# Loads of keys, values and weights issued as two halves: partitions 0 to 63 by SyncE, 64 to 127 by ScalarE

## The chip, the core and the metric

The kernel runs on one core of a Trainium2 chip. The metric is device time in microseconds; the kernel before takes 1985.83 us, the median of three runs.

## What is computed

One decode step goes through four attention layers, A, B, A, B, each added to a running x of 640 values. A and B have their own caches and weights, and in A the repetition of heads is 1, so both compute the same:

```python
q = (layernorm(x) @ wq).reshape(1, 1, 32, 192).transpose(0, 2, 1, 3)
scores = einsum("bhqd,bhkd->bhqk", q, k_cache) * 192 ** -0.5   # k_cache: 1 x 32 x 8192 x 192
p = softmax(scores, axis=-1)
o = einsum("bhqk,bhkd->bhqd", p, v_cache)
x = x + o.transpose(0, 2, 1, 3).reshape(1, 1, 32 * 192) @ wo   # wq 640 x 6144, wo 6144 x 640
```

All inputs are bf16. Each cache has 100.7 MB (32 x 8192 x 192 x 2 bytes), each weight 7.9 MB. Both caches of A and of B are read twice, once for each layer that uses them, but for a few parts that stay on the chip between two layers.

## The kernel before

Heads are worked in pairs, 16 pairs to a layer. A pair's keys lie in the on-chip memory as 128 partitions: 0 to 63 hold the first head, 64 to 127 the second, and each partition holds 128 positions of 192 values, a contiguous row of 49152 bytes in DRAM too. Values lie likewise. The buffer `pool` is cut into eight slots of 24576 bytes per partition (NSLOT), so that a pair's keys or values take two slots (a "whole" load of 6144 KB, line 369), or one for each half (3072 KB, line 371).

For each pair, VectorE multiplies the keys with the query (line 543, into the place of the keys), TensorE sums the products over the 192 values by matmuls with an identity (lines 556 and 58, into S), VectorE reduces the rest (565) and finds the maximum (567, 574), ScalarE takes the exponentials (580), TensorE multiplies with the values (620 and 58, into OY), VectorE gathers the result (638, 639), TensorE sums it into one row (650), and ScalarE writes that row, divided by the sum of exponentials (661). ScalarE also copies the query of the next pair (502). After five, ten and fifteen pairs TensorE multiplies the output rows with a part of wo (513).

The program is written for each engine as a `Queue`: a list of waits and instructions in order, put out at the end (lines 708 to 713). Each engine works through its own list in order. An operation returns an event, a semaphore and the count it will have reached, and others wait for that. Loads come from the list `plan`. `ahead()` (line 394) is called after each step of the computation: it takes loads from the plan as long as the instructions that free their slots have already been put into TensorE's list (`freed`), and `transfer` (336) puts each into SyncE's list, `SP`, with a wait for those instructions. So all 181 loads go through SyncE's one queue, in the order of the plan, and each raises its slot's semaphore `semS` by 16 when it has landed. One small transfer is ScalarE's: x (line 410), the first instruction of its list. The result goes out by SyncE (line 704).

Of the kernel before, what the change touches and what calls it, by code (L numbers as in the profile page):

```python
# [63 lines left out]
PAIRS_W = 5  # L64
# [4 lines left out]
def build(nc, A_x, A_k, A_v, A_wq, A_wo, B_x, B_k, B_v, B_wq, B_wo, out):  # L69
    _, H, SK, DH = A_k.shape  # L70
    D = A_x.shape[-1]
    P = 128
    J = 2 * SK // P
    JU = J // 2
    DC = D // P
# [6 lines left out]
    PD = 2 * DH  # L82
    NW = PAIRS_W * PD // P
    QC = (NPAIR - 1) * PD
    QR = QC // 3
    TS = JU * DH
    QW = H * DH
    Q_PARTS = [(0, 2), (2, 2), (4, 1)]
    OI = PD // P
    NB = [0, 5, 0, 5]  # L90
# [4 lines left out]
                    wo=[NPAIR - PAIRS_W, 1, 1 + PAIRS_W], wol=0)  # L95
    ORDER = [FORWARD, FORWARD, FORWARD, BACKWARD]

    with ExitStack() as ctx:
        def sb(name, shape, dt):
            return ctx.enter_context(nc.sbuf_tensor(name, shape, dt))  # L100
# [4 lines left out]
        def sem(name):  # L105
            return ctx.enter_context(nc.semaphore(name))

        ident = sb("ident", [P, P], BF16)
        pool = sb("pool", [P, NSLOT * TS], BF16)
        slot = [pool[:, i * TS:(i + 1) * TS] for i in range(NSLOT)]  # L110
        wq0 = [sb(f"wq0{i}", [P, DC, PD], BF16) for i in range(2)]
        rows = sb("rows", [P, QR], BF16)
# [52 lines left out]
        AC = Queue(sem("pACT"))  # L165
        PO = Queue(sem("pPOOL"))
        SP = Queue()
        semS = [sem(f"semS{i}") for i in range(NSLOT)]
        semOL, semOB, semVQ, semX, semOUT = [sem(n) for n in ("semOL", "semOB", "semVQ", "semX", "semOUT")]

        e = PO.op(lambda g: g.memset(ident[:], 0.0))
# [5 lines left out]
        e = PO.op(lambda g: g.memset(mask, 0.0))  # L177
        for t in range(G):
            e = PO.op(lambda g, t=t: g.affine_select(
                out=mask, in_=mask, compare_op=ALU.not_equal, fill=1.0,  # L180
                base=-32 * t, pattern=[[-1, 2], [-2, VK]], channel_multiplier=1), e)
# [10 lines left out]
        def pair(l, p):  # L192
            return ORDER[l]["pairs"][p]
# [11 lines left out]
        def whole(kind, l, p):  # L205

            if kind == "t":
                return False
            if kind == "k":
                return l < 2 and p not in (PAIRS_W, 2 * PAIRS_W) or l == 3 and p > 1  # L210
            if p == NPAIR - 1:
                return False
            return l != 2 or p not in (0, PAIRS_W, 2 * PAIRS_W)
# [7 lines left out]
        for l in range(NL):  # L221
# [8 lines left out]
            for p in range(NPAIR):  # L230
# [17 lines left out]
                if p < NPAIR - 2:  # L248
                    if first_load("v", l, p) == (l, p):
                        plan += [("v", l, p, u) for u in range(2)]  # L250
                        if l == 2 and p == 1:
                            i = plan.index(("k", l, 1, 0))
# [31 lines left out]
        place, before, holder = {}, {}, [None] * NSLOT  # L284
# [40 lines left out]
        def wq_rows(l, g):  # L325

            c0, k = Q_PARTS[g]
            if l < 2:
                i = place[("wq", l, 0)] * TS
                return pool[:, i + c0 * QW:i + (c0 + k) * QW].rearrange("p (c n) -> p c n", c=k)  # L330
            return slot[place[("wq", l, g)]][:, 0:k * QC].rearrange("p (c n) -> p c n", c=k)

        def quarters(n):
            return n[0] == "v" and n[2:] == (NPAIR - 1, 1) and NB[n[1]] > 0

        def transfer(n):
            l = n[1]
            o = ORDER[l]
            w = W[l % 2]
            free = [freed[b] for b in before[n]]  # L340
            if n[0] == "wol":
                r0 = o["wol"] * PD
                return SP.op(lambda s: s.dma_start(
                    rows[:], w["wo"][r0:r0 + PD].rearrange("(p i) n -> p (i n)", p=P)),
                    *free, sem=semOL, inc=16)
            if n[0] == "t":
                return max(free, key=lambda e: e[1]) if free else None
            if n[0] == "wob":
                r0 = o["wo"][2] * PD
                return SP.op(lambda s: s.dma_start(  # L350
                    slot[place[("wo", l, 2)]][:, (NW - NB[l]) * D:NW * D],
                    w["wo"][r0:r0 + PAIRS_W * PD].rearrange("(p i) n -> p (i n)", p=P)[:, (NW - NB[l]) * D:]),
                    sem=semOB, inc=16)
            if n[0] == "vq":
                n = ("v", l, NPAIR - 1, 1)
            i = place[n]
            t = slot[i]
            if n[0] in "kv":
                h = 2 * pair(l, n[2])
                r = w[n[0]][0, h:h + 2].rearrange("h (p j) d -> (h p) (j d)", j=J)  # L360
                if quarters(n):
                    x = TS // 2
                    if n in landed:
                        return SP.op(lambda s: s.dma_start(t[:, x:], r[:, TS + x:]), sem=semVQ, inc=16)
                    return SP.op(lambda s: s.dma_start(t[:, 0:x], r[:, TS:TS + x]), *free, sem=semS[i], inc=16)
                if whole(*n[:3]):
                    if n[3] == 1:
                        return landed[n[:3] + (0,)]
                    f = lambda s: s.dma_start(pool[:, i * TS:(i + 2) * TS], r)
                else:  # L370
                    f = lambda s: s.dma_start(t, r[:, n[3] * TS:(n[3] + 1) * TS])
            elif n[0] == "wq" and l < 2:
                f = lambda s: s.dma_start(pool[:, i * TS:i * TS + DC * QW], w["wq"].rearrange("(p c) n -> p (c n)", c=DC))
            elif n[0] == "wq":
                c0, k = Q_PARTS[n[2]]
                f = lambda s: s.dma_start(
                    wq_rows(l, n[2]),
                    w["wq"][:, o["q1"] * PD:o["q1"] * PD + QC].rearrange("(p c) n -> p c n", c=DC)[:, c0:c0 + k, :])
            else:
                r0 = o["wo"][n[2]] * PD  # L380
                k = NW - NB[l] if n[2] == 2 else NW
                f = lambda s: s.dma_start(
                    t[:, 0:k * D], w["wo"][r0:r0 + PAIRS_W * PD].rearrange("(p i) n -> p (i n)", p=P)[:, 0:k * D])
            return SP.op(f, *free, sem=semS[i], inc=16)

        def need(n):

            while n not in landed:
                m = plan[issued[0]]
                issued[0] += 1  # L390
                landed[m] = transfer(m)
            return landed[n]

        def ahead():

            while issued[0] < len(plan):
                m = plan[issued[0]]
                if any(b not in freed for b in before[m]):
                    return
                issued[0] += 1  # L400
                landed[m] = transfer(m)
# [300 lines left out]
        for l in range(NL):  # L702
            ev_z, ev_true = layer(l, ev_z, ev_true)
        e = SP.op(lambda s: s.dma_start(out[0, 0].rearrange("(p c) -> p c", c=DC), x_bf[:]), ev_true, sem=semOUT, inc=16)
        SP.wait(e)
# [10 lines left out]
def bass_interleave_layers__gqa_block_cached__mha_block_cached__decode_kernel(  # L716
    nc: bass.Bass,
    A_x: bass.AP,
    A_k_cache: bass.AP,
    A_v_cache: bass.AP,  # L720
    A_wq: bass.AP,
    A_wo: bass.AP,
    B_x: bass.AP,
    B_k_cache: bass.AP,
    B_v_cache: bass.AP,
    B_wq: bass.AP,
    B_wo: bass.AP,
    out: bass.AP,
):
    build(nc, A_x, A_k_cache, A_v_cache, A_wq, A_wo, B_x, B_k_cache, B_v_cache, B_wq, B_wo, out)  # L730
# [28 lines left out]
```

## Time and profile before

| What | Value |
|---|---|
| Median of three runs | 1985.83 us (1985.55 to 1986.44) |
| The profiled execution's own time | 1985.81 us |
| Its span, first to last instruction | 1984.0 us |
| Mean granted TensorE clock | 0.776 |
| Bytes moved, mean rate | 849.25 MB, 428 GB/s |
| VectorE multiplication of keys (L543) | 512 of 1753 ns, 861.2 us |
| TensorE sums (L58, into S) | 2944 of 425 ns, 789.1 us |
| ScalarE exponentials (L580) | 128 of 435 ns, 55.7 us |

The span is the time within which instructions ran; the profiled execution's own time is 1.8 us more. A busy time is the sum over an engine's instructions. Engines overlap, so these times don't add up to the span. In the groups, "out<-in" names the buffers written and read; SPq and ACTq are the sequencers of SyncE and ScalarE, where loads are issued. In a row of 40 digits each digit is the busy share of a fortieth of the span, in tenths.

### The profile page before, as it was taken

The page shows a single profiled execution, that of the slowest core. Times are in us where ns is not written, and L with a number is a line of the kernel's source. Part 1 is how long each engine was busy: PE and PEld are TensorE (multiplying, and loading weights), DVE is VectorE, ACT ScalarE, POOL GpSimd, SP SyncE. Part 2 cuts the span into 40 slices and gives each one's busy share as a digit, 9 for nine tenths or more (in the row PEclk, how much of TensorE's full clock was granted, in tenths as well). Part 3 has the DMA queues.
Part 4 walks back from the last instruction along what each step waited for, and adds up shares of the span by engine and source line. Part 5 has one row for each costly group of instructions (what it writes and reads, how often), then busy time and mean ns, then how long its engine had stood idle before and what let it go on. Part 6 is the DMA issues. An engine that isn't in the chain of part 4 may idle for free.

```text
span 1984.0 us, 13908 instructions
## 1 busy us (share of the span) xinstructions
PE 1273.4 (64%) x8310; PEld 150.1 (8%) x3266; DVE 1200.7 (61%) x1371; ACT 139.5 (7%) x461; POOL 4.5 (0%) x22
## 2 busy tenths in 40 slices
PE   3567567566466666665775665675676766656657
PEld 0001001000200100100020010010002001001001
DVE  3566467467166656556745565665664775665665
ACT  0000000000000000000010000000000000000000
POOL 0000000000000000000000000000000000000000
PEclk9787777777587787777876777878886887777777
DMA  9999999999999999999999999999999999999998
GB/s 412 438 430 431 431 437 429 431 430 431 433 435 431 432 429 436 430 431 432 427 388 433 430 430 430 432 430 430 431 431 427 435 432 434 430 432 432 432 431 353
DMA packets 26926, 849.25 MB, mean 428 GB/s; under 512 B 3184, under 2 KB 3184, under 8 KB 3952
## 3 DMA queue, kind: packets, MB, share of 16 engines
q1 hardware_dynamic: 26720, 848.38, 99.5%
q8 instruction: 45, 0.74, 0.2%
q14 instruction: 17, 0.14, 0.0%
q10 hardware_dynamic: 144, 0.00, 0.0%
HBM read 848.36 MB, written 0.00 MB: 428 GB/s over the span
## 4 chain that ended last, share of the span: by engine, by line
DMA 68%; DVE 15%; PE 15%; ACT 1%; issue 0%; SPq 0%
DMA pool<-in_B_k_cache_dram 27%; DMA pool<-in_A_v_cache_dram 20%; DMA pool<-in_A_k_cache_dram 14%; DVE pool L543 13%; PE S L58 6%; PE OY L58 5%; DMA pool<-in_B_v_cache_dram 4%; PE OY L620 3%; DMA pool<-in_B_wo_dram 2%; ACT p_sb L580 1%; DVE acc L639 1%; DMA pool<-in_A_wq_dram 1%; DVE s_sb L565 1%; PE OY L513 0%; PE S L556 0%
## 5 line engine op out<-in xcount | busy, mean ns | idle before, releaser
L543 DVE TENSOR_TENSOR pool<-pool,q_sb 128x3072 bf16<-128x3072 bf16 x512 | 861.2, 1753 | 241.5 <-DMA pool<-in_B_k_cache_dram 144.0
L58 PE MATMUL S<-pool,ident 128*128 128x512 bf16 x2944 | 789.1, 425 | 20.3 <-DVE pool L543 19.0
L650 PE MATMUL TB<-acc,small 128*1 128x192 f32 x240 | 82.1, 493 | 219.1 <-DVE acc L639 219.1
L556 PE MATMUL S<-pool,ident 128*128 128x512 bf16 x128 | 62.9, 491 | 213.6 <-DVE pool L543 213.6
L58 PE MATMUL OY<-pool,p_sb 128*16 128x512 bf16 x1920 | 197.0, 485 | 0.0
L638 DVE TENSOR_SCALAR acc<-OY,small 128x192 f32<-128x192 f32 x64 | 26.7, 418 | 274.2 <-PE OY L58 246.2
L620 PE MATMUL OY<-pool,p_sb 128*16 128x512 bf16 (+1 forms) x1216 | 147.5, 497 | 62.7 <-DMA pool<-in_A_v_cache_dram 56.4
L639 DVE SCALAR_TENSOR_TENSOR acc<-OY,small,acc 128x192 f32<-128x192 f32 x424 | 177.1, 418 | 14.9
L565 DVE TENSOR_REDUCE s_sb<-S 128x64 f32<-128x512 f32 x128 | 88.1, 688 | 69.4 <-PE S L58 69.4
L502 ACT ACTIVATE q_sb<-QM 128x192 bf16<-128x192 f32 x60 | 19.9, 331 | 954.8 <-PE QM L496 954.8
L661 ACT ACTIVATE rows<-TB,small 1x192 bf16<-1x192 f32 x120 | 43.2, 406 | 585.1 <-PE TB L650 585.1
L634 DVE RECIPROCAL small<-TB 1x2 f32<-1x2 f32 x64 | 11.2, 175 | 96.7 <-PE TB L595 75.2
L580 ACT ACTIVATE p_sb<-s_sb,small 64x128 bf16<-64x128 f32 x128 | 55.7, 435 | 161.9 <-DVE small L574 161.1
L556 PEld LDWEIGHTS S<-pool,ident 128*128 128x128 bf16 x128 | 13.0, 101 | 686.2 <-DVE pool L543 636.4
L595 PE MATMUL TB<-small,ones 128*1 128x2 f32 x120 | 11.4, 165 | 74.1 <-ACT p_sb L580 74.1
L620 PEld LDWEIGHTS OY<-pool,p_sb 128*16 128x16 bf16 (+1 forms) x1216 | 39.3, 107 | 203.6 <-issue 133.5
L570 PE MATMUL QM<-ident,m_bf 128*64 128x64 bf16 x128 | 14.1, 217 | 54.4 <-DVE m_bf L567 53.8
L650 PEld LDWEIGHTS TB<-acc,small 128*1 128x1 f32 x240 | 19.7, 101 | 311.4 <-DVE acc L639 283.9
L513 PE MATMUL OY<-oT,pool 128*128 128x1 bf16 x900 | 38.2, 178 | 3.5 <-ACT oT L528 2.8
L513 PEld LDWEIGHTS OY<-oT,pool 128*128 128x128 bf16 x900 | 37.1, 131 | 7.0 <-ACT oT L528 3.6
L574 DVE TENSOR_REDUCE small<-QM 128x1 f32<-128x64 f32 x64 | 14.4, 225 | 36.1 <-PE QM L570 36.1
L496 PEld LDWEIGHTS QM<-rows,one_b 1*64 1x64 bf16 x120 | 6.2, 100 | 350.7 <-issue 344.8
(59 smaller groups left out, 186.1 us busy)
## 6 DMA issues: line engine op xcount, KB each, us to landing
pool<-in_B_k_cache_dram SPq DMA_DIRECT2D x28, 6144.0 KB, 38.1
pool<-in_B_v_cache_dram SPq DMA_DIRECT2D x28, 6144.0 KB, 34.2
pool<-in_A_v_cache_dram SPq DMA_DIRECT2D x27, 6144.0 KB, 27.6
pool<-in_A_k_cache_dram SPq DMA_DIRECT2D x34, 3072.0 KB, 20.4
pool<-in_A_k_cache_dram SPq DMA_DIRECT2D x14, 6144.0 KB, 36.8
pool<-in_A_v_cache_dram SPq DMA_DIRECT2D x10, 3072.0 KB, 14.3
pool<-in_B_k_cache_dram SPq DMA_DIRECT2D x8, 3072.0 KB, 22.7
pool<-in_A_wo_dram SPq DMA_DIRECT2D x6, 2400.0 KB, 21.4
```

Source lines behind the costliest of these rows:

```text
L58: return t.add_instruction(mybir.InstMatmult(name=t.bass.get_next_instruction_name(), engine=mybir.EngineType.PE, ins=[t.lower_ap(rhs), t. ...
L502: lambda a: a.activation(q_sb[i][:], QM[:, 0:DH], ACT.Copy), e, last["q"][i], bank=QMu)
L513: e = PE.op(lambda t, i=i, c=c, f=y_first[0], fin=n[0] == "wol" and i == k - 1: t.matmul(YB[:, c:c + 1], lhsT=t3[:, i, c:D:DC], rhs=o[:, i ...
L543: e = DV.op(lambda v, d0=d0: v.tensor_tensor(k3[:, :, d0:d0 + QD], kin[:, :, d0:d0 + QD], q_sb[qi][:, d0:d0 + QD].unsqueeze(1).broadcast_t ...
L556: t.matmul(S[:, :], lhsT=ident[:], rhs=k3[:, :, d0:d0 + R], start=True, stop=fin) if d0 == 0 else
L565: lambda v, u=u: v.tensor_reduce(s[:, u * JU:(u + 1) * JU], SP_[u][:].rearrange("p (j r) -> p j r", r=R), AX.X, ALU.add), ev_S[p, u], last ...
L580: ev_p[p] = AC.op(lambda a, h=h, r=r: a.activation(p_sb[par][r, :, h], s[r, :], ACT.Exp, bias=negm[par][r, 0:1], accum_out=l_col[par][r, h ...
L620: t.matmul(o, lhsT=x, rhs=y, start=f, stop=fin) if c == 0 else
L638: v.tensor_scalar(acc[:], O[:, 0:DH], pick[:, 0:1], None, ALU.mult) if i == 0 else
L639: v.scalar_tensor_tensor(out=acc[:], in0=O[:, i * DH:(i + 1) * DH], scalar=pick[:, i:i + 1], in1=acc[:], op0=ALU.mult, op1=ALU.add)), e if ...
L650: e = PE.op(lambda t, h=h: t.matmul(TB[96:97, C_O + h * DH:C_O + (h + 1) * DH], lhsT=half[:, h:h + 1], rhs=acc[:], start=True, stop=True), ...
L661: last["TO"] = last["row_written"] = AC.op(lambda a, h=h: a.activation(orow[:, o0 + h * DH:o0 + (h + 1) * DH], TB[96:97, C_O + h * DH:C_O ...
```

## The change

`transfer` gets a helper, `move`, that issues a load twice: partitions 0 to 63 on SyncE's list and 64 to 127 on ScalarE's. Both get the waits that the one had, and both raise the same semaphore by 16, so the event returned has a count of 32 for each load; for that the two lists share their table of counts. All kinds of loads are changed in the same way: keys, values, wq, and the four forms of wo. x and the result go as before. The order of the instructions on TensorE, VectorE and GpSimd is unchanged; ScalarE's list has the 181 issues in between its activations, at the places where `ahead()` is called.

```diff
+        SP.counts = AC.counts
...
             free = [freed[b] for b in before[n]]
+
+            def move(dst, src, sem):
+
+                for q, r in (SP, slice(0, P // 2)), (AC, slice(P // 2, P)):
+                    e = q.op(lambda s, r=r: s.dma_start(dst[r], src[r]), *free, sem=sem, inc=16)
+                return e
+
             if n[0] == "wol":
                 r0 = o["wol"] * PD
-                return SP.op(lambda s: s.dma_start(
-                    rows[:], w["wo"][r0:r0 + PD].rearrange("(p i) n -> p (i n)", p=P)),
-                    *free, sem=semOL, inc=16)
+                return move(rows, w["wo"][r0:r0 + PD].rearrange("(p i) n -> p (i n)", p=P), semOL)
...
                 if whole(*n[:3]):
                     if n[3] == 1:
                         return landed[n[:3] + (0,)]
-                    f = lambda s: s.dma_start(pool[:, i * TS:(i + 2) * TS], r)
+                    f = pool[:, i * TS:(i + 2) * TS], r
                 else:
-                    f = lambda s: s.dma_start(t, r[:, n[3] * TS:(n[3] + 1) * TS])
+                    f = t, r[:, n[3] * TS:(n[3] + 1) * TS]
...
-            return SP.op(f, *free, sem=semS[i], inc=16)
+            return move(*f, semS[i])
```

The other branches (`wq`, the parts of `wo`, the quarters of the last values) are rewritten in the same form.

More of the change, by code (lines that the diff above doesn't have):

```diff
@@ L349, in transfer @@
                 r0 = o["wo"][2] * PD
[L350 to L353, printed above, removed]
+                return move(slot[place[("wo", l, 2)]][:, (NW - NB[l]) * D:NW * D],
+                            w["wo"][r0:r0 + PAIRS_W * PD].rearrange("(p i) n -> p (i n)", p=P)[:, (NW - NB[l]) * D:], semOB)
             if n[0] == "vq":
@@ L363, in transfer @@
                     if n in landed:
-                        return SP.op(lambda s: s.dma_start(t[:, x:], r[:, TS + x:]), sem=semVQ, inc=16)
-                    return SP.op(lambda s: s.dma_start(t[:, 0:x], r[:, TS:TS + x]), *free, sem=semS[i], inc=16)
+                        free = []
+                        return move(t[:, x:], r[:, TS + x:], semVQ)
+                    return move(t[:, 0:x], r[:, TS:TS + x], semS[i])
                 if whole(*n[:3]):
@@ L368, in transfer @@
                         return landed[n[:3] + (0,)]
-                    f = lambda s: s.dma_start(pool[:, i * TS:(i + 2) * TS], r)
+                    f = pool[:, i * TS:(i + 2) * TS], r
                 else:
-                    f = lambda s: s.dma_start(t, r[:, n[3] * TS:(n[3] + 1) * TS])
+                    f = t, r[:, n[3] * TS:(n[3] + 1) * TS]
             elif n[0] == "wq" and l < 2:
-                f = lambda s: s.dma_start(pool[:, i * TS:i * TS + DC * QW], w["wq"].rearrange("(p c) n -> p (c n)", c=DC))
+                f = pool[:, i * TS:i * TS + DC * QW], w["wq"].rearrange("(p c) n -> p (c n)", c=DC)
             elif n[0] == "wq":
                 c0, k = Q_PARTS[n[2]]
-                f = lambda s: s.dma_start(
-                    wq_rows(l, n[2]),
-                    w["wq"][:, o["q1"] * PD:o["q1"] * PD + QC].rearrange("(p c) n -> p c n", c=DC)[:, c0:c0 + k, :])
+                f = (wq_rows(l, n[2]),
+                     w["wq"][:, o["q1"] * PD:o["q1"] * PD + QC].rearrange("(p c) n -> p c n", c=DC)[:, c0:c0 + k, :])
             else:
@@ L381, in transfer @@
                 k = NW - NB[l] if n[2] == 2 else NW
-                f = lambda s: s.dma_start(
-                    t[:, 0:k * D], w["wo"][r0:r0 + PAIRS_W * PD].rearrange("(p i) n -> p (i n)", p=P)[:, 0:k * D])
-            return SP.op(f, *free, sem=semS[i], inc=16)
+                f = t[:, 0:k * D], w["wo"][r0:r0 + PAIRS_W * PD].rearrange("(p i) n -> p (i n)", p=P)[:, 0:k * D]
+            return move(*f, semS[i])
         def need(n):
```

## The prediction

> **What bounds the kernel now.** I read the summary first, then the queues, the chain, single loads and the first microseconds. The page's busy shares and slices:
>
> ```profile
> PE 1273.4 (64%) x8310; PEld 150.1 (8%) x3266; DVE 1200.7 (61%) x1371; ACT 139.5 (7%) x461; POOL 4.5 (0%) x22
> ...
> DMA  9999999999999999999999999999999999999998
> GB/s 412 438 430 431 431 437 429 431 430 431 433 435 431 432 429 436 430 431 432 427 388 433 430 430 430 432 430 430 431 431 427 435 432 434 430 432 432 432 431 353
> ...
> q1 hardware_dynamic: 26720, 848.38, 99.5%
> q8 instruction: 45, 0.74, 0.2%
> ...
> q10 hardware_dynamic: 144, 0.00, 0.0%
> ```
>
> No engine is busy over 64%, while the DMA row is full in every slice and nearly every slice moves 430 GB/s. q1 is SyncE's queue (all keys, values, weights), q10 ScalarE's (only x). The chain of waits, and the loads' times to landing:
>
> ```profile
> DMA 68%; DVE 15%; PE 15%; ACT 1%; issue 0%; SPq 0%
> ...
> pool<-in_B_k_cache_dram SPq DMA_DIRECT2D x28, 6144.0 KB, 38.1
> pool<-in_B_v_cache_dram SPq DMA_DIRECT2D x28, 6144.0 KB, 34.2
> ...
> x_bf<-in_A_x_dram ACTq DMA_DIRECT2D x1, 1.2 KB, 21.6
> ```
>
> A 6144 KB load needs 6.29 MB / 432 GB/s = 14.6 us, yet lands 34 to 38 us after issue: it lies behind one or two others. So the queue holds over 20 us of work when a load is issued, and a microsecond of delay in issuing costs nothing. The stretches show the same rate away from the ends (columns: stretch, length, busy us of each engine, TensorE clock, DMA share, GB/s):
>
> ```profile
> 100.00:500.00 400.00, 263.02 (x1618) 26.33 (x562) 254.85 (x283) 27.77 (x97) 0.00 (x0) 0.76 1.00 431
> 500.00:1000.00 500.00, 309.62 (x2059) 35.79 (x797) 300.12 (x341) 33.84 (x113) 0.55 (x1) 0.77 1.00 432
> ...
> 1934.00:1984.00 50.00, 37.13 (x330) 9.27 (x216) 29.16 (x34) 3.47 (x13) 0.00 (x0) 0.80 0.83 353
> ```
>
> The kernel is a stream of 849.25 MB. At 432 GB/s that is 1966 us; the other 18 us of the 1984.0 us span are the start, the dip at the third layer (388) and the tail (353). What counts is what the change does to the rate.
>
> [...]
> 1. [...] its packet records have 49152-byte packets of 1.82 us, 27.0 GB/s per engine, 432 from 16. It has no transfer of 64 partitions.
> 2. [...]
> 3. [...] 144 packets of x are 16 x 9, eight rows and a completion on each engine.
> 4. [...] x, 1.2 KB, landed only after 21.6 us, nine of its tiny packets behind nine large ones (8 x 61440 bytes at 2.27 us are 18.1 us, after some 3 us of start).
>
> **The change part by part.**
>
> *Issues.* Each of the 181 loads becomes two, 181 more issues, on ScalarE. In the stretch of the first microseconds an issue takes 0.33 to 0.42 us:
>
> ```profile
> 0.73 0.40 ACTq L410 DMA_DIRECT2D x_bf<-in_A_x_dram  x1
> ...
> 0.74 0.38 SPq L373 DMA_DIRECT2D pool<-in_A_wq_dram  x1
> ...
> 1.18 0.42 SPq L369 DMA_DIRECT2D pool<-in_A_k_cache_dram  x1
> ...
> 32.76 0.33 SPq L369 DMA_DIRECT2D pool<-in_A_v_cache_dram  x1
> ```
>
> 181 x 0.35 = 63 us on ScalarE, busy 139.5 of 1984: hidden; uncovered it would be at most 63 us. SyncE issues as often as before. Completion packets double (16 x 181 more of 9 ns, so 181 x 9 ns = 1.6 us per engine): +2 us.
>
> *Waits.* ScalarE now also waits until TensorE has freed the slots. Behind those waits in its order stand the exponentials (L580), query copies (L502) and output rows (L661), for which TensorE and VectorE wait. But a transfer is only put in once the instruction that frees its slot has been put in, and the ScalarE work that follows waits for later TensorE instructions: after the wait for a value product comes an output row, whose own matmul (L650) follows that product. TensorE runs in order, so the new wait is over first. Cost 0; if an exponential did come behind an issue without slack, 64 pairs x 0.4 = 26 us, under the prefetch anyway.
>
> *Start.* x (nine packets per engine) is now ahead of the upper half of wq in one queue, so that half comes after eight large SyncE packets: at full rate 4 x 2.27 + 4 x 1.82 = 16.4 us, then its own 4 x 2.27 = 9.1, plus some 3 us: wq lands near 29 instead of 22 us. The loads issued by then (wq and the first keys, 14.2 MB) keep the engines busy to about 36; the next issue, at 32.76 before, goes to about 37 to 39, a gap of 3 us; if the upper half then goes alone at half rate, up to 15 us. At half rate throughout there is no gap, since those 14.2 MB last 65 us. So 0 to 15; in the main case 0.
>
> *Rate.* This decides. [...] All engines begin with the SyncE queue and take the queues in turn with packets of equal size, so they are on the same half together: [...] then they change over. [...] Bounds: 849.25 MB / 216 = 3932 us (always in step), and 1966 (always opposite). [...] in the packet records the 16 completions of one load lie 0.6 to 5 us apart, after the first loads 1.2 to 1.8. That would loosen the step, but a load is complete only with its slowest engine, and pairs that get ahead run out of packets (eight slots, some three loads ahead) and start the next load in step again. So the closest pair sets the pace: I take d = 0.15 us, 0.15 / 3.64 = 4%: 3932 x 0.96 = 3775.
>
> *Sum.* 3775 + 18 of ends + 2 of completions + 0 for issues and waits = 3795 us of span, + 1.81 that lies around it in the profiled execution (1985.81 against 1984.0; the median, 1985.83, is the same) = 3797, rounded to **3800**. Own range 3400 (d = 0.5 us) to 4000 (d = 0 gives 3954; the rest for slower packets). VectorE (1200.7) and TensorE (1273.4) have room at that pace, so nothing else comes late.
>
> **The rivals.**
> - *Out of step.* [...] offsets are anywhere in a packet: 1.5 x 1966 + 22 = 2971, **2970**, from 2300 to 3400. For it: the spread of 5 us late in the trace, over two packets. Against: running dry puts pairs in step again.
> - *[...] only the start is late.* If the halves go to different engines, or the two queues settle on opposite halves, 432 GB/s stay, with +3 us of start, +2 of completions: **1991**[...]. [...]
> - *Faster.* The other side: engines with two queues to draw on. [...] Its place is the gap between 428 GB/s (mean) and 432, 18 us, of which the last slice keeps 0.17 x 50 = 8.5: at most some 10 us, **1976**. [...] Against: DMA share 1.00 already.
> - *That the change doesn't do what it says* is excluded by the instruction order: every load stands as 64 rows on both queues; TensorE and VectorE keep their order.
>
> **How the numbers follow.** In step 0.62; out of step 0.18; [...] 0.14 (half of it within 0.2%); faster 0.05; beyond 4000, 0.01. The range 2300 to 4000 holds the first two, 0.80. A change of 0.2% (4 us) is about what measurement tells here: slower 0.62 + 0.18 + 0.07 + 0.01 = 0.88, same 0.07, faster 0.05.
>
> **What would show it.** Right: mean GB/s near 220 to 230 with the DMA row still full; q1 and q10 each near half the bytes; 49152-byte packets about twice 1.82 us; time to landing doubled; busy VectorE and TensorE as before in us, near 32% in share. Out of step: packets between 1.82 and 3.64, GB/s near 290. Wrong: packets at 1.82 us with 430 GB/s. If GB/s falls while packets stay at 1.82 us and the DMA share falls, ScalarE's waits starve the queue and my zero for them fails.

## The result

The changed kernel takes 3615.64 us (median of four runs, 3564.14 to 3685.89), the kernel before 1985.74 us in the same session: 1.80 times as long (95% interval 1.792 to 1.806, for the runs nearest the fastest; the median of all four is 1.82 times). Its executions differ by 3.4% among themselves, those of before by 0.05%. The profiled execution took 3580.12 us, its span 3578.3 us. On its page the busy times, the slices and the queues read:

```profile
PE 1386.4 (39%) x8310; PEld 154.2 (4%) x3266; DVE 1202.9 (34%) x1371; ACT 139.7 (4%) x461; POOL 4.5 (0%) x22
...
DMA  9999999999999999999999999999999999999997
GB/s 211 218 212 216 220 215 217 222 219 223 228 231 229 232 245 246 261 253 246 237 224 229 223 226 237 252 241 252 255 245 247 255 242 249 256 258 264 269 289 197
DMA packets 29824, 849.28 MB, mean 237 GB/s; under 512 B 6080, under 2 KB 6080, under 8 KB 6848
...
q1 hardware_dynamic: 14880, 424.19, 49.6%
q10 hardware_dynamic: 14880, 424.19, 49.6%
```

VectorE works as long as before, in us; its share has fallen only since the span is longer. The DMA row is as full as before, yet moves 55% as much (237 against 428 GB/s on average): the engines are hardly ever without packets, the packets take longer. TensorE's 9% more go with its lower granted clock (0.656 against 0.776). Each queue has half the bytes. The rate starts at half of before and climbs, with a fall in the middle. Waits and issues:

```profile
another core or an unknown queue 36%; DMA 26%; DVE 19%; PE 17%; ACT 1%; issue 1%; ACTq 0%; DVEq 0%
...
pool<-in_B_k_cache_dram SPq DMA_DIRECT2D x28, 3072.0 KB, 59.4
pool<-in_B_k_cache_dram ACTq DMA_DIRECT2D x28, 3072.0 KB, 77.1
...
x_bf<-in_A_x_dram ACTq DMA_DIRECT2D x1, 1.2 KB, 1.7
```

In the chain, "another core or an unknown queue" is most likely loads too, since the kernel has one core; together with "DMA" it is 62%. Why the profile can't name their queue isn't known. Time to landing has grown to 1.6 times on SyncE and twice on ScalarE, though each load has half the bytes. That ScalarE's half of these loads lands some 18 us later after its issue than SyncE's isn't explained here.

In the stretches (columns as in the prediction: stretch, length, busy us by engine, clock, DMA share, GB/s) the climb and the fall are seen:

```profile
150.00:700.00 550.00, 190.74 (x1138) 20.61 (x436) 169.47 (x191) 19.67 (x69) 0.00 (x0) 0.64 1.00 217
...
1500.00:1850.00 350.00, 138.07 (x778) 12.70 (x264) 127.93 (x138) 13.71 (x48) 0.00 (x0) 0.66 1.00 243
1850.00:1900.00 50.00, 27.47 (x221) 5.99 (x143) 18.93 (x22) 1.89 (x7) 0.00 (x0) 0.64 0.87 217
...
3000.00:3500.00 500.00, 202.68 (x1236) 21.66 (x459) 183.72 (x208) 20.72 (x72) 0.00 (x0) 0.67 1.00 266
```

Away from the ends, the DMA share drops only at 1850 us, between two layers (0.87). In the packet records the mean 49152-byte packet takes 3.67 us from 50 to 150 us, twice the 1.82 of before; it falls to 3.1 by 1500 us, is 3.3 again from 1700 to 1850 us, 3.62 around 2000 us, and 2.8 near the end.

The records also give each packet's queue, so one can count how many of the 16 engines are on SyncE's half and how many on ScalarE's. From 50 to 150 us at least 15 engines are on the same half for 78% of the time, and they change over together, after one packet or two. This share falls to 1% from 1700 to 1850 us, is 27% again just after the pause (1950 to 2050 us), and 0% from 3300 to 3500 us. So the engines start in step and drift apart, and after the pause they are nearer to in step again. That packets had grown from 3.1 to 3.3 us before the pause, with the engines not in step, isn't explained by it.

### The profile page after: what moved, and what is told of

Read it like the earlier page. It is cut to its first block, busy times and chain, and to the rows that moved or that the text cites. A ratio compares the mean times of both kernels' runs of the same rounds, so it can differ in the third digit from the quotient of the medians.

```text
span 3578.3 us, 14095 instructions
## 1 busy us (share of the span) xinstructions
PE 1386.4 (39%) x8310; PEld 154.2 (4%) x3266; DVE 1202.9 (34%) x1371; ACT 139.7 (4%) x461; POOL 4.5 (0%) x22
## 4 chain that ended last, share of the span: by engine, by line
another core or an unknown queue 36%; DMA 26%; DVE 19%; PE 17%; ACT 1%; issue 1%; ACTq 0%; DVEq 0%
DVE pool L546 13%; DMA pool<-in_A_k_cache_dram 10%; DMA pool<-in_A_v_cache_dram 8%; PE S L58 8%; PE OY L58 4%; DVE acc L642 4%; PE OY L623 3%; DMA pool<-in_B_wq_dram 2%; DMA pool<-in_A_wq_dram 2%; DMA pool<-in_B_k_cache_dram 1%; ACT p_sb L583 1%; DMA pool<-in_B_wo_dram 1%; DVE s_sb L568 1%; DMA rows<-in_A_wo_dram 1%
## 5 line engine op out<-in xcount | busy, mean ns | idle before, releaser
L58 PE MATMUL S<-pool,ident 128*128 128x512 bf16 x2944 | 826.0, 443 | 11.7 <-DVE pool L546 11.0
L559 PE MATMUL S<-pool,ident 128*128 128x512 bf16 x128 | 68.0, 532 | 1048.6 <-DVE pool L546 1048.5
L623 PE MATMUL OY<-pool,p_sb 128*16 128x512 bf16 (+1 forms) x1216 | 166.3, 574 | 650.7 <-DMA pool<-in_A_v_cache_dram 417.7
L58 PE MATMUL OY<-pool,p_sb 128*16 128x512 bf16 x1920 | 232.1, 577 | 0.0
```

Of the source, the lines that this page charges most:

```text
L58: return t.add_instruction(mybir.InstMatmult(name=t.bass.get_next_instruction_name(), engine=mybir.EngineType.PE, ins=[t.lower_ap(rhs), t. ...
L559: t.matmul(S[:, :], lhsT=ident[:], rhs=k3[:, :, d0:d0 + R], start=True, stop=fin) if d0 == 0 else
L623: t.matmul(o, lhsT=x, rhs=y, start=f, stop=fin) if c == 0 else
```

## The experiments

The theory is that of the prediction: all engines are on the same half of the partitions at a time, and packets to one half alone take about twice as long (in the changed kernel, with 15 or more engines on one half for 78% of the time, 3.67 us against 1.82). The rivals: two queues cost as such; ScalarE's waits starve the loads; 64 rows are slow as such.

**Both halves by one queue.** 4016.11 us (two runs), 2.02 times the kernel before.

```diff
-                for q, r in (SP, slice(0, P // 2)), (AC, slice(P // 2, P)):
+                for q, r in (SP, slice(0, P // 2)), (SP, slice(P // 2, P)):
```

> Both halves of each load go by SyncE's queue, lower half first; ScalarE issues only x. [...] still half rate, and slower than the changed kernel if anything, because with one queue the halves change only every four packets[...]: 3650 to 3950 us, 49152-byte packets near 3.6 us. Rival, two queues cost (an engine that changes from queue to queue loses time): about 1990 us, packets 1.82 us. Rival, ScalarE's waits starve the loads: about 1990 us too.

The line of its page on packets:

```profile
DMA packets 29824, 849.27 MB, mean 212 GB/s; under 512 B 6081, under 2 KB 6081, under 8 KB 6849
```

Without a second queue and without any wait on ScalarE it is slower still: neither rival can be why the changed kernel is slow. It is over the range I gave, since packets of engines that are all on one half take 3.84 us (the median in the records), not 2 x 1.82 = 3.64.

**Halved along the row.** 2000.52 us, 1.0069 (1.0052 to 1.0086) of before.

```diff
-                for q, r in (SP, slice(0, P // 2)), (AC, slice(P // 2, P)):
-                    e = q.op(lambda s, r=r: s.dma_start(dst[r], src[r]), *free, sem=sem, inc=16)
+                n2 = dst.shape[-1] // 2
+                for q, r in (SP, slice(0, n2)), (AC, slice(n2, 2 * n2)):
+                    e = q.op(lambda s, r=r: s.dma_start(dst[..., r], src[..., r]), *free, sem=sem, inc=16)
```

> Each load is still issued twice, on the same two queues, with the same waits, but halved along the row: all 128 partitions, first half of the row by SyncE, second half by ScalarE. [...] 432 GB/s and 1980 to 1995 us; 24576-byte packets at 0.91 us. Rivals of two queues or of ScalarE's waits: as slow as the changed kernel, 3500 us or more.

```profile
DMA packets 53504, 849.28 MB, mean 425 GB/s; under 512 B 6080, under 2 KB 7104, under 8 KB 11712
...
q1 hardware_dynamic: 26720, 424.19, 49.9%
q10 hardware_dynamic: 26720, 424.19, 49.8%
```

As many issues, the same two queues, the same waits on ScalarE: 0.7% remain of 80%, 5 us over the range I gave. And these are packets: in the records they fill 1995 of 1999.1 us, before 1977 of 1984.0; two packets of 24576 bytes take 2 x 0.917 us, one of 49152 1.82. ScalarE's exponentials wait 160.7 us for VectorE, 161.1 before.

**One queue, 64 rows of two kinds.** Only partitions 0 to 63, or only 32 to 95, are loaded after the fourth pair: 2101.84 against 1695.38 us (one run each).

```diff
-                for q, r in (SP, slice(0, P // 2)), (AC, slice(P // 2, P)):
-                    e = q.op(lambda s, r=r: s.dma_start(dst[r], src[r]), *free, sem=sem, inc=16)
+                r = slice(0, 64) if n[0] in "kv" and l * NPAIR + n[2] >= 4 else slice(0, P)   # or slice(32, 96)
+                e = SP.op(lambda s, r=r: s.dma_start(dst[r], src[r]), *free, sem=sem, inc=16)
```

> One queue. From the fifth pair on keys and values are loaded for partitions 0 to 63 alone; the upper 64 are left as they were, so half of the keys' and values' bytes are left out (some 480 of 849 MB are moved). [...] 370 MB at 216 GB/s and 109 MB at 432, 1713 + 252 = 1965 us, as long as the whole; packets of 49152 bytes near 3.6 us. If the rows of a load don't matter for its rate: 480 MB at 432 GB/s would take 1110 us, and the computation decides, 1350 to 1600 us.

> As the run on partitions 0 to 63, with the same bytes left out, but partitions 32 to 95 are loaded. [...] full rate, 480 MB in 1110 us, so the computation decides: 1350 to 1600 us, packets of 49152 bytes near 1.82 us. If 64 rows are slow as such (fewer rows per engine, more completions): like the other run, about 1965 us.

Slices and queue of the run on 0 to 63:

```profile
GB/s 419 431 345 223 206 204 226 207 206 216 272 208 208 220 205 209 219 204 208 207 266 209 202 226 211 203 226 208 207 224 270 204 200 232 204 206 226 208 204 186
...
q1 hardware_dynamic: 17312, 480.33, 99.2%
```

and of the run on 32 to 95:

```profile
GB/s 409 436 434 379 298 261 258 284 270 272 271 336 261 255 288 296 246 260 296 189 294 359 242 237 324 243 245 315 251 259 367 282 259 332 227 244 330 229 300 31
...
q1 hardware_dynamic: 17312, 480.33, 70.1%
```

The same rows in number, bytes and packets, and in DRAM both are 64 neighbouring rows of 49152 bytes; what differs is the partitions that they are written to. On 0 to 63 the rate falls to some 205 GB/s as soon as whole loads end, with the queue full (99.2%); more than half the bytes take longer than all of them did. On 32 to 95 the engines are done with time to spare (70.1%), their median 49152-byte packet takes 1.82 us, and the computation decides: in the chain of this run VectorE has the most.

```profile
DVE 58%; PE 29%; DMA 8%; ACT 4%; issue 2%; SPq 0%; ACTq 0%; DVEq 0%
```

It took 1695 us where I had guessed 1600 at most. So it is which partitions, not how many. Most of the 137 us over the first forecast are again the 3.84 us: 370 MB at 205 GB/s + 252 = 2057 us.

**Whole loads on two queues.** Keys and weights by SyncE, values by ScalarE: 2034.39 us, 1.0247 (1.0230 to 1.0264).

```diff
-                for q, r in (SP, slice(0, P // 2)), (AC, slice(P // 2, P)):
-                    e = q.op(lambda s, r=r: s.dma_start(dst[r], src[r]), *free, sem=sem, inc=16)
-                return e
+                q = AC if n[0] == "v" else SP
+                return q.op(lambda s: s.dma_start(dst[:], src), *free, sem=sem, inc=16)
```

> Two queues, nothing split: keys and weights as whole loads of 128 partitions by SyncE, values as whole loads by ScalarE, with the same waits. [...] as many packets as before, 1983 to 1992 us. If the 14 us that the split along the row cost came from its many packets, nothing of them is left here (within 4 us of the kernel before); if they came from having two queues, or from ScalarE's waits, about 2000 us here too.

```profile
1000.00:1500.00 500.00, 320.77 (x2055) 37.65 (x815) 291.86 (x337) 34.53 (x115) 0.55 (x1) 0.77 0.96 406
...
1980.00:2030.00 50.00, 28.66 (x293) 9.15 (x213) 20.98 (x28) 3.46 (x13) 0.00 (x0) 0.70 0.55 231
```

A miss, for a reason none of the cases had. Packets take as long as before (median 1.82 us), but they fill only 1983 of 2030.6 us: the engines idle for 48 us instead of 7. Shown is that they run dry, mostly in the third layer and at the end. It may come from two queues that no longer keep the plan's order between keys and values, or from the values' issues standing behind other work in ScalarE's order; neither was tried.

**The border moved.** 3872.23 us (two runs) on two queues.

```diff
-                for q, r in (SP, slice(0, P // 2)), (AC, slice(P // 2, P)):
+                for q, r in (SP, slice(32, 96)), (AC, slice(96, P)), (AC, slice(0, 32)):
```

> The changed kernel with the border moved: SyncE loads partitions 32 to 95, ScalarE loads 96 to 127 and 0 to 31 as two transfers. [...] in turn that is one packet at 1.82 us for each at 3.64: 1.5 x 1966 + 22 = 2970 us in step, somewhat less out of step, 2700 to 3000. If two queues or 64 rows are slow as such: as the changed kernel, 3500 us or more.

The expectation failed: it is no faster than the changed kernel. In the records SyncE's packets of 49152 bytes, forecast at 1.82 us, take 2.76 us on average in the first 50 us and 3.2 to 3.5 us afterwards. To see whether it came from the two queues, the same three transfers went by SyncE alone, in the same order: 3951.62 us (two runs).

> The three transfers of the run with the border moved (32 to 95, 96 to 127, 0 to 31), now all on SyncE's one queue, so that engines stay within a few us of each other and can't be on transfers of different queues. [...] 4 packets at 1.82 us and 4 shared at 3.84, on average 2.83 us, 1.555 x 1966 + 22 = 3080 us, 2950 to 3350. If transfers of 32 rows, or 64 rows across the border, are slow as such: 3800 us or more, as with two queues.

Failed too, but its stretches tell when:

```profile
0.00:50.00 50.00, 8.75 (x74) 2.27 (x29) 4.91 (x19) 3.56 (x3) 2.79 (x19) 0.97 0.98 268
50.00:100.00 50.00, 19.25 (x106) 1.32 (x28) 18.76 (x21) 2.03 (x7) 0.00 (x0) 0.67 1.02 265
100.00:500.00 400.00, 138.48 (x780) 12.69 (x266) 128.04 (x139) 13.68 (x48) 0.00 (x0) 0.64 1.00 227
...
1000.00:2000.00 1000.00, 307.65 (x1786) 28.81 (x603) 279.21 (x307) 32.37 (x107) 0.00 (x0) 0.62 0.99 200
```

For 100 us it is near what was expected (2.83 us per packet would be 278 GB/s). Half of the packets go to 32 to 95. In the records, which don't name the transfer, 132 of the 382 packets of 49152 bytes from 15 to 100 us take 1.7 to 1.9 us and 170 take 3.5 to 3.9; the rest lie mostly between. The short ones are most likely those to 32 to 95 (1.82 us in the run on these alone), the long ones those of 32 rows. If so, 64 rows across the border aren't slow as such, and 32 rows are no slower than 64 on one half (3.84 us). Then it gets worse (200 GB/s from 1000 to 2000 us): 5% of the 49152-byte packets take 4.76 us or more, longer than the 3.84 us of a stream to one half. What makes them so long wasn't shown.

**Does an offset between engines help?** Each half in four, then in two pieces along the row, issued in turn by the two queues: 3171.65 us (two runs) and 3357.12 us (1.692, interval 1.688 to 1.697).

```diff
-                for q, r in (SP, slice(0, P // 2)), (AC, slice(P // 2, P)):
-                    e = q.op(lambda s, r=r: s.dma_start(dst[r], src[r]), *free, sem=sem, inc=16)
+                m = dst.shape[-1] // 4          # or // 2
+                for c in range(4):              # or range(2)
+                    for q, r in (SP, slice(0, P // 2)), (AC, slice(P // 2, P)):
+                        e = q.op(lambda s, r=r, c=c: s.dma_start(
+                            dst[r][..., c * m:(c + 1) * m], src[r][..., c * m:(c + 1) * m]), *free, sem=sem, inc=16)
```

> The changed kernel with each half cut into four transfers along the row: packets of 12288 instead of 49152 bytes, eight transfers for each load. [...] the same offsets of some tenths of a us to some us now span a whole turn of two packets (2 x 0.46 us), so they are anywhere in it: 1.5 x 1966 = 2950 us, plus some 80 us for four times as many packets, up to 3500 if the closest pair of engines still sets the pace. So more and smaller transfers would be faster than the changed kernel. If offsets don't matter: slower than the changed kernel, 3690 us or more.

> The changed kernel with each half cut into two transfers along the row, packets of 24576 bytes. [...] in the changed kernel its few 24576-byte packets took 1.58 us, two of them 3.16 against 3.33 for one of 49152, so 3616 x 3.16 / 3.33 = 3430 us, 3300 to 3550, between the changed kernel and the one in four pieces (3172). If offsets don't matter: not faster than 3616.

Four times the transfers and 12% faster than the changed kernel; two pieces lie between, and both runs lie in the ranges given. Then the four pieces with both halves on SyncE's queue (`(SP, slice(P // 2, P))` in the loop): 3167.77 us, median of five runs from 3091.61 to 3381.71.

> One queue as in the first run (4016 us), but each half cut into four transfers along the row, lower and upper in turn. Each engine then changes from half to half every four packets of 12288 bytes, that is every 49152 bytes, as the changed kernel does with its two queues. If the relief comes once a changeover[...], the number of queues doesn't matter and this takes as long as the changed kernel: 3500 to 3750 us. If smaller packets are what made the run in four pieces fast: near 3170. If two queues are what makes the changed kernel faster than one: near 4000.

By its total the expectation failed. But the profiled execution (3381.71 us, the longest of the five) has in its stretches:

```profile
0.00:150.00 150.00, 42.50 (x234) 4.06 (x65) 39.09 (x53) 6.90 (x15) 2.81 (x19) 0.75 1.00 217
...
1500.00:1690.00 190.00, 94.52 (x543) 6.94 (x146) 95.01 (x108) 11.13 (x39) 0.00 (x0) 0.74 1.01 337
1690.00:1720.00 30.00, 13.22 (x193) 8.62 (x193) 9.64 (x18) 0.87 (x3) 0.55 (x1) 0.50 0.92 233
...
1750.00:1900.00 150.00, 54.48 (x286) 3.62 (x77) 47.99 (x55) 4.78 (x16) 0.00 (x0) 0.63 1.02 229
```

It starts where the changed kernel starts, climbs to 337 GB/s, and where the engines ran dry for a moment (DMA share 0.92) it is back at 229.

The table compares the starts, from the packet records between 50 and 150 us. Relief is what is missing to 3.84 us for 49152 bytes, the time of packets when all engines stay on one half (in the run on 0 to 63 packets of 24576 and 12288 bytes take a median 1.91 and 0.955 us, a half and a quarter of it). With two queues the changeovers are counted in the records; with one they follow from the order of the issues.

| Run | us per 49152 bytes | changeovers in 49152 bytes | relief each, us |
|---|---|---|---|
| one queue | 3.79 | 1/4 | 0.05 x 4 = 0.20 |
| changed kernel | 3.67 | 0.78 | 0.17 / 0.78 = 0.22 |
| one queue, four pieces | 3.60 | 1 | 0.24 |
| two pieces | 2 x 1.79 | 1.52 | 0.26 / 1.52 = 0.17 |
| four pieces | 4 x 0.804 | 4 | 0.62 / 4 = 0.16 |

The relief of one changeover lies between 0.16 and 0.24 us, while the changeovers differ sixteenfold: at the start, the relief goes by changeovers. These are single executions; one with the layout of the third row (the next run) gives 0.18. What differs between the runs later is how fast the rate climbs, and why it is faster in some isn't known.

**Running dry on purpose.** The last kernel with a wait after every tenth load, until it has landed: 3896.94 us (3894.04 and 3899.83).

```diff
+                turns[0] += 1
+                if turns[0] % 10 == 0:
+                    SP.wait(e)
```

> The run on one queue in four pieces (3168 us), with one thing added: after every tenth load SyncE waits until that load has landed, so that all engines run out of packets some 18 times and start again together. If engines drift apart and are put in step again whenever they run dry (in the profile of that run the rate rose from 217 to 337 GB/s and fell back to 229 where they had run dry), the rate stays at the 217 to 224 GB/s of its first 700 us: 849 MB / 220 = 3860 us and some 18 x 3 us of gaps with 20 us of ends, 3850 to 4000 us. If running dry doesn't matter, only the gaps are added: about 3240 us.

Its slices:

```profile
GB/s 211 216 217 221 221 211 224 219 212 222 216 217 218 217 222 213 224 223 213 219 223 222 222 222 230 211 227 217 215 223 223 219 207 220 218 213 225 216 216 203
```

As expected by the theory: the rate never rises, and 729 us are added where the gaps, by my estimate, account for some 54 (18 of 3 us; the one in the stretches above, a DMA share of 0.92 over 30 us, is 2.4 us). The two runs agree within 0.15%, where the kernel without the waits spread over 9%. So what makes these kernels faster than twice the time builds up while the engines are busy, and running dry clears it. That it is offsets between engines fits the counts in the changed kernel (15 or more engines on one half for 78% of the time, and 3.67 us a packet, at the start; 0% and 2.83 us near the end). How an offset shortens the packets wasn't shown.

## Why the prediction was right, and where its sizes were off

- *What bounds it, and the rate.* Right: a stream at its limit, and at the start half the rate of before (219 GB/s from 50 to 150 us against 432), with the engines on one half at a time. Shown by the pair of 64-row runs (same bytes, other partitions, 2101.84 against 1695.38 us), by the two ways to halve a load (along the row 1.007, across partitions 1.80) and by the 78% of the time with 15 or more engines on one half. That engines take the queues in turn shows in the packet records of before (16 packets of wq first; from 4.6 us on a 10-byte packet of x, 9 ns, goes ahead of each 61440-byte one of wq, 2.27 us). That they change over after each packet holds for the run in four pieces; the changed kernel's stay for one packet or two. That one half alone gets half the rate was an assumption when the prediction was made, as nothing in the run of before shows it; the prediction's 216 GB/s, half of the 432 measured there, is not quite reached: 205 GB/s once only 0 to 63 are loaded.
- *The size.* The term "3932 x 0.96 = 3775" is off in both factors. A packet takes 3.84 us and not 2 x 1.82 = 3.64 when all engines stay on one half, which alone would be +5%. And d, what an offset between engines takes off a packet's time, was an estimate, near 0.15 us only at the start (3.84 - 3.67 = 0.17); over the whole run the mean 49152-byte packet took 3.33 us, so d = 3.84 - 3.33 = 0.51 us on average. 1966 x 3.33 / 1.82 = 3597 us, against a span of 3578. The errors partly cancel, so that 3800 came within 5% of 3616 is in part luck.
- *The step that failed inside it:* that engines which get ahead run dry and are put in step again, so that those closest in step hold d near 0.15 us. Running dry does take the gain away (3168 to 3897 us by forcing it), but in the profile of the changed kernel it happens once away from the ends, after 1850 us, so the offsets grow for more than a thousand us. Its rival "out of step" (2970 us) describes where this drift leads: its factor 1.5, also an estimate, is 2.73 us a packet, and from 3300 to 3500 us the mean is 2.83. The kernel lies between the two, nearer to the first.
- *What drives the drift* wasn't shown by any run here.
- *Issues and waits at nothing.* Right: with both in place and all 128 partitions in each transfer, 1.007 remains, and packets account for it. An issue took a median 0.50 us on ScalarE rather than 0.35, 95 us in all instead of 63, hidden all the same.
- *Start.* Wrong in detail, without consequence: SyncE's first issue took 0.56 us instead of 0.38, and x, most likely for that reason, got through ahead of the large packets and landed after 1.7 us. Nothing gained, since wq landed only at 44.6 us.
- *The rival "faster".* Nothing of it: no run on two queues came under the kernel before, and the best of them was 0.7% above it.

## What to carry to other kernels

When a stream of loads fills the DMA engines, look at which partitions each transfer reaches, not at how many queues issue it: a full DMA row at 237 GB/s instead of 428, with packets of 3.33 us instead of 1.82, was here the sign that the engines were on one half of the partitions together. Keep all 128 partitions in each transfer; if a load must be cut in two, cut it along the row (here 1.007 of before, against 1.80 across partitions). Whole loads spread over two queues by kind, which gives up the order between them, cost more here (2.5%) than twice the packets (0.7%); why is open.

## What was not expected of the hardware

- A stream to partitions 0 to 63 alone takes 5% more than twice the time: 49152 bytes in 3.84 us instead of 2 x 1.82 = 3.64, some 205 GB/s instead of 216.
- Running dry takes a gained rate away: it grows while the engines are busy (217 to 337 GB/s in 1690 us) and falls back with one short pause (to 229). So a kernel became slower by pausing (3168 to 3897 us), and another faster by issuing four times as many transfers (3616 to 3172 us).
- With work on two queues the engines of the changed kernel changed over together, after one packet or after two (22 changeovers from 50 to 150 us, at 3.67 us a packet).
- An issue of 64 rows took a median 0.47 us on SyncE and 0.50 on ScalarE; one of 128 rows took 0.33, and 0.33 and 0.36 when the loads were halved along the row on the same two queues. So the difference goes with the rows, not with the second queue.
